# Moving one gradient store, three partial-partition stores and one weight load in a traffic-bound attention backward kernel

## The chip, the cores and the metric

The kernel runs on one core of a Trainium2 chip. The metric is the device time of one execution in microseconds (us), as the median of several runs. Each run is also told with its *span*, the time from the first to the last instruction by the profiler, about 1.8 us less than the device time.

In the profile PE is the matmul engine, DVE the vector engine, ACT the scalar engine, POOL GpSimd and SP SyncE. SPq and ACTq are the queues on which SyncE and ACT issue DMAs, and L546 is line 546 of that kernel. `[t <-DMA x]` tells that the engine stood idle for t us before, until that DMA. The *DMA engines* are the 16 units that move the bytes. A *semaphore* is a counter on which instructions wait.

A ratio below is the mean time of one kernel's runs over that of the kernel before in the same rounds on the same chip, so it is not quite the ratio of the medians that are quoted beside it. The kernel before was run 6, 11, 11, 11 and 9 times in five sessions (the last four on different chips), with medians of 404.82, 404.98, 404.67, 404.64 and 404.92 us and single runs from 403.89 to 407.32 us. Differences under about 0.2% (0.8 us) are therefore near the noise, and the text says so where it matters. Ratios of different sessions are compared with the same caution.

## The reference, cut to what matters

The reference computes a gated mix of a one-token attention over a cache and a small MLP, and all gradients of it. Shapes are of one token: x has 640 elements, there are 32 heads, and each head has a K cache and a V cache of 4096 x 128 in bfloat16 (1 MiB each).

```
q  = x @ wq                       # wq: 640 x 4096
p  = softmax(q . K / sqrt(128))   # per head
o  = p . V
a  = o @ wo                       # wo: 4096 x 640
b  = mish(x @ w1 + b1) @ w2       # w1: 640 x 1728
out = g * a + (1 - g) * b,        g = sigmoid(sum(x * gate_w))
# returned: out and the gradients of x, K, V, wq, wo, w1, b1, w2, gate_w
```

Every gradient has the shape of its input. So the kernel reads all of K, V and the weights (82.03 MB) and writes as much again. Each row of dK is a number times q, and each row of dV a number times a vector, so the arithmetic is light. The kernel is a copy machine with some work in the middle.

## The kernel before

Loads of K and V, and of the weights, are issued from SyncE (a hardware queue, q1 in the profile). Nearly all stores are issued from GpSimd (a software queue, q0), the last ones from SyncE. These are the parts that the change and the argument touch.

```
def ring(h):                                   # who issues the dK and dV stores
    return nc.sync if h >= H - 2 else nc.gpsimd
def load_wq(w):                                # a quarter of wq, 1280 KB
    ...
    nc.sync.dma_start(wqs[w][:], wq_v[...])

# start: wq piece 0, wo piece 0, K0, V0, K1, V1, wo piece 1, w1, ... all on SyncE
load_wq(0); load_wo(0); load_k(0); load_v(0); ...

def dwo():                                     # gradient of wo for four heads
    ...
    (nc.sync if g == NG - 1 else nc.gpsimd).dma_start(dwo_v[g], wos[g][:])

def dw1_part(rc):                              # gradient of w1, written over w1
    def f():
        nc.vector.tensor_scalar(w1_sb[:, rc, :], m["dh_bc"][:], x_f[:, rc:rc + 1], None, ALU.mult)
        if rc == RC - 1:
            nc.gpsimd.dma_start(dw1_v, w1_sb[:])          # 2160 KB
    return f

# in dv_half(h, 1): the store of dV of head h
if h % 10 == 9:
    spread(h // 10, dVv[h], st["dV"])          # heads 9, 19, 29
else:
    ring(h).dma_start(dVv[h], st["dV"][:])     # 128 partitions, 8 KB each

def spread(i, dst, t):                         # one dV store in three pieces
    ...
    if i == 0:
        nc.gpsimd.inc_swdge_sem([], [], mode="reset_dge_cursor")
    for a, b in (((120, 125), (0, 120), (125, 128)),
                 ((0, 14), (14, 119), (119, 128)),
                 ((0, 8), (8, 128)))[i]:
        nc.gpsimd.dma_start(out[a:b, :], src[a:b, :], max_dma_last_dim=J * Dh)

# the head loop: loads run three heads ahead
load_k(h + 3); load_v(h + 3); ...; period(h)
...
# after the last head: last pieces of dwq
nc.sync.dma_start(dwq_v[:, :, CL:], dwq_l[:])
```

`spread` needs a word. By the general rule of the Trainium skill ("DMA: Bandwidth & Descriptors", Why a DMA increments its semaphore by 16 and not by 1), a store of 128 partitions is divided over all 16 DMA engines, so 8 rows each, and a software-queue store whose partition count is divisible by 15 and not by 16 runs on 15 consecutive engines from a cursor that goes round. The page also has an exception for some direct copies on trn2. The pieces are cut so that the 120-row (or 105-row) piece leaves out the same engine each time. By the general rule the left-out engine gets 2, 2 and 1 rows in place of 8 from the three patterns, so 19 rows less in all. That is an estimate from the page's rule.

Of the kernel before, what the change touches and what calls it, by code (L numbers as in the profile page):

```python
# [16 lines left out]
def kernel(  # L17
# [24 lines left out]
    nc = tc.nc  # L42
    P = 128
    _, H, Sk, Dh = A_k_cache.shape
# [3 lines left out]
    RC = D // P  # L48
# [4 lines left out]
    WG = 8  # L53
# [14 lines left out]
    dVv = out_3.rearrange("b h (p j) d -> (b h) p j d", p=P)  # L68
    wq_v = A_wq.rearrange("(rc r) c -> r rc c", r=P)
# [4 lines left out]
    dw1_v = out_6.rearrange("(rc r) f -> r rc f", r=P)  # L74
# [38 lines left out]
    kts, vts, wqs, wos = {}, {}, {}, {}  # L113

    def ring(h):
        return nc.sync if h >= H - 2 else nc.gpsimd

    def load_k(h):
        if h < H:
            kts[h] = kv_in.tile([P, J, Dh], BF16, name="Kn", tag="Kn", bufs=KB)  # L120
            nc.sync.dma_start(kts[h][:], Kv[h])

    def load_v(h):
        if h < H:
            vts[h] = kv_in.tile([P, J, Dh], BF16, name="Vn", tag="Vn", bufs=VB)
            nc.sync.dma_start(vts[h][:], Vv[h])

    def load_wq(w):
        if w < H // WG:
            wqs[w] = wts.tile([P, RC, WG * Dh], BF16, name="wq_g", tag="wq_g")  # L130
            nc.sync.dma_start(wqs[w][:], wq_v[:, :, w * WG * Dh:(w + 1) * WG * Dh])

    def load_wo(g):
        if g < NG:
            wos[g] = wts.tile([P, G, D], BF16, name="wo_g", tag="wo_g", bufs=3)
            nc.sync.dma_start(wos[g][:], wo_v[g])
# [3 lines left out]
    def load_w2(c):  # L140
        a, b = CH[c][0], min(CH[c][1], FM)
        w2cs[c] = mlp.tile([P, 5, D], BF16, name="w2c", tag="w2c", bufs=2)
        nc.sync.dma_start(w2cs[c][:, 0:b - a, :], w2_v[:, a:b, :])

    load_wq(0)
    load_wo(0)
    load_k(0)
# [4 lines left out]
    w1_sb = mlp.tile([P, RC, F], BF16, name="w1_sb", tag="w1_sb")  # L152
# [94 lines left out]
    steps, done = [], {}  # L247

    def add(name, kind, fn, deps=(), head=0):
        steps.append((name, kind, fn, tuple(deps), head))  # L250
# [154 lines left out]
    def mlp_steps():  # L405
# [136 lines left out]
        def dw1_part(rc):  # L542
            def f():
                nc.vector.tensor_scalar(w1_sb[:, rc, :], m["dh_bc"][:], x_f[:, rc:rc + 1], None, ALU.mult)
                if rc == RC - 1:
                    nc.gpsimd.dma_start(dw1_v, w1_sb[:])  # L546
            return f

        H0 = 2
# [55 lines left out]
    def s_chunk(h, c, ts):  # L605
        gp = gps[h // G]
        if c == 0:
            sts[h] = {"A": sa_ps.tile([P, 512], F32, name="sA", tag="sA")}
        products(sts[h]["A"][:, 0:J + W], ts[c], c, gp["x2"][:, 0, h % G])

    def outer(dst, col, row, half):
        n = J // 2
        a, b = half * n, (half + 1) * n
        nc.vector.tensor_tensor(  # L614
            dst[:, a:b, :].rearrange("p j (a b) -> p j a b", b=2),
            col[:, a:b, :].unsqueeze(2).to_broadcast([P, n, Dh // 2, 2]),
            row.rearrange("p (a b) -> p a b", b=2).unsqueeze(1).to_broadcast([P, n, Dh // 2, 2]),
            ALU.mult)
# [16 lines left out]
    def dv_half(h, half):  # L635
        st = sts[h]
        if half == 0:
            st["dV"] = outs.tile([P, J, Dh], BF16, name="dV_sb", tag="dVK")
        outer(st["dV"], st["p"], gps[h // G]["qd"][:, 1, (h % G) * Dh:(h % G + 1) * Dh], half)
        if half == 1:  # L640
            if h % 10 == 9:
                spread(h // 10, dVv[h], st["dV"])
            else:
                ring(h).dma_start(dVv[h], st["dV"][:])  # L644

    def spread(i, dst, t):
        src = t[:].rearrange("p j d -> p (j d)")
        out = dst.rearrange("p j d -> p (j d)")
        if i == 0:
            nc.gpsimd.inc_swdge_sem([], [], mode="reset_dge_cursor")  # L650
        for a, b in (((120, 125), (0, 120), (125, 128)), ((0, 14), (14, 119), (119, 128)), ((0, 8), (8, 128)))[i]:
            nc.gpsimd.dma_start(out[a:b, :], src[a:b, :], max_dma_last_dim=J * Dh)

    def period(h):
# [12 lines left out]
        def o_part(a, b):  # L667
            for j in range(a, b):
# [31 lines left out]
        nc.vector.scalar_tensor_tensor(pj[:], in0=DP[:, 0:J], scalar=1.0, in1=e[:], op0=ALU.mult, op1=ALU.mult,  # L700
                                       accum_out=part[:])
        dv_half(h, 0)
        nc.tensor.transpose(PT, part[:].to_broadcast([P, P]), ident_f[:])  # L703
        if nxt:
# [6 lines left out]
        nc.vector.scalar_tensor_tensor(ds[:], in0=DP[:, 0:J].unsqueeze(2).to_broadcast([P, J, 2]), scalar=dd[:], in1=p_bf[:],  # L711
                                       op0=ALU.subtract, op1=ALU.mult)
        dv_half(h, 1)
        nc.vector.tensor_scalar(o_all[:, h:h + 1], O[:, 0:1], rz[:], None, ALU.mult)  # L714
        if nxt:
# [19 lines left out]
    dwqt = {}  # L735
    CL = (NG - 1) * GD

    def dwq_make(rc):
        def f():
            t = dwqt[rc] = kv_in.tile([P, J * Dh], BF16, name="dwq_t", tag="Kn" if rc % 2 == 0 else "Vn", bufs=KB)  # L740
            nc.vector.tensor_scalar(t[:, 0:CL], dq_bc[:, 0:CL], x_f[:, rc:rc + 1], None, ALU.mult)
        return f

    def dwq_store(rc):
        (nc.sync if rc else nc.gpsimd).dma_start(dwq_v[:, rc, 0:CL], dwqt[rc][:, 0:CL])
# [8 lines left out]
            s_chunk(0, c - 1, tk)  # L754
    s_chunk(0, NT - 1, tk)
    mlp_steps()
    for h in range(H):
        hh, g = h % G, h // G
        if hh == 3:
            assert g == 0 or f"dwo{g - 1}" in done  # L760
            load_wo(g + 2)
            if g % 2 == 0:
                assert g == 0 or f"dx{RC - 1}_{g - 1}" in done
                load_wq(g // 2 + 1)
        load_k(h + 3)
        load_v(h + 3)
        if hh == 1 and g + 1 < NG:
            rest = steps[:]
            steps.clear()
            prep_steps(g + 1, h)  # L770
            steps.extend(rest)
        if h == H - 3:
            for rc in range(RC):
                add(f"dwq{rc}", "D", dwq_make(rc), (f"dqb{NG - 2}",), h + (rc + 1) // 2)
                add(f"dwqs{rc}", "T", lambda rc=rc: dwq_store(rc), (f"dwq{rc}",), h)
        period(h)
        if hh == G - 1:
            mlp_left = steps[:]
            steps.clear()
            finish_steps(g)  # L780
            steps.extend(mlp_left)
# [7 lines left out]
    for rc in range(RC):  # L789
        nc.vector.tensor_scalar(dwq_l[:, rc, :], dq_bc[:, CL:], x_f[:, rc:rc + 1], None, ALU.mult)  # L790
    nc.sync.dma_start(dwq_v[:, :, CL:], dwq_l[:])
    assert len(dwqt) == RC

    C = lambda name, shape, dt=F32: const.tile(list(shape), dt, name=name)
# [64 lines left out]
```

## Time and profile before

| what | before |
|---|---|
| median of 3 runs, known when the prediction was made (of all 6 of that session) | 405.26 us (404.82) |
| span of the profiled run | 402.6 us |
| bytes moved, mean rate | 164.93 MB, 410 GB/s |
| PE, DVE, ACT busy | 75%, 75%, 44% of the span |

The page of the kernel before, rows of DMA: the busy share of the 16 engines in 40 slices of the span (9 is 90% or more), the rate in each, and the queues with packets, MB and their share of the 16 engines' time.

```profile
DMA  8999999999999999999999999999999999999995
GB/s 290 420 413 408 422 424 418 419 426 421 423 424 419 395 421 414 421 425 423 423 419 425 425 423 416 412 425 423 421 425 422 424 420 424 424 415 367 413 396 216
...
q1 hardware_dynamic: 16480, 91.20, 54.9%
q0 software_dynamic: 11216, 72.85, 43.7%
```

The DMA row is full from the second slice to the last but one, while no computing engine is above 75%. The kernel is bound by traffic. The dips are the first slice (290), the 37th (367) and the last two (396, 216).

The chain of waits of the kernel before, near its end (start, length, what):

```profile
332.40 0.67 POOL out_dram L631
...
333.25 0.89 POOL out_dram L546
...
336.80 25.24 DMA out_dram<-dV_sb
...
362.13 1.23 DVE dK_sb L614
```

Two lines of its table of waits (who waited for whom: us in total, times, longest), and one of the same table for SyncE's queue:

```profile
PE qc_ps L278 <- DMA wq_g<-in_A_wq_dram: 6.9, 2, 4.8
...
DVE dK_sb L614 <- DMA out_dram<-dV_sb: 3.8, 1, 3.8
```

```profile
SPq L375 <- DMA out_dram<-dV_sb: 4.9, 1, 4.9
```

L546 is the dw1 store. It is issued at 333.25 us, and the dV store behind it on the same queue, issued at 336.80 us, lands only 25 us later. DVE then finds no free output buffer and stands for 3.8 us. SyncE holds the last dwo store (L375) for 4.9 us until another store lands.

The timeline of SyncE's queue in the kernel before, from 370 us on (start, length, engine, line, what), and below it DVE's instructions that make the data of the last two stores.

```profile
370.18 0.35 SPq L644 DMA_DIRECT2D out_dram<-dV_sb  x1
...
379.46 0.33 SPq L644 DMA_DIRECT2D out_dram<-dV_sb  x1
...
391.42 0.33 SPq L375 DMA_DIRECT2D out_dram<-wo_g  x1
393.60 0.38 SPq L791 DMA_DIRECT2D out_dram<-dwq_l  x1
```

### The profile page before, as it was taken

The numbers are of one execution on the slowest core, as the hardware profiler recorded it, in microseconds if no ns is written. First come the engines' busy times: TensorE is split into PE (matmuls) and PEld (weight loads), VectorE is DVE, ScalarE is ACT, GpSimd is POOL, SyncE is SP. The second block draws the span as 40 slices with busy tenths as digits, with TensorE's granted clock in tenths as the row PEclk, the third lists the DMA queues.
The fourth block names the chain that finished last, engine by engine and source line by source line (L and its number), as shares of the span: only waits on it lengthen the run. The fifth ranks groups of instructions, "written<-read, shape, count | busy, mean of one in ns | idle before, by whom it ended". The sixth has DMA issues, their size and how long they took to land.

```text
span 402.6 us, 13606 instructions
## 1 busy us (share of the span) xinstructions
PE 300.7 (75%) x5872; PEld 271.9 (68%) x5872; DVE 303.7 (75%) x791; ACT 177.6 (44%) x411; POOL 46.5 (12%) x93
## 2 busy tenths in 40 slices
PE   0688888678888788878876988739887888966510
PEld 0577888568877778778866878628776778856500
DVE  3339666646599999977669799855999996968980
ACT  1355455325453555546523556505554555533300
POOL 0001111010011311111101113101111112121000
PEclk9999999857999999989988899957999999998755
DMA  8999999999999999999999999999999999999995
GB/s 290 420 413 408 422 424 418 419 426 421 423 424 419 395 421 414 421 425 423 423 419 425 425 423 416 412 425 423 421 425 422 424 420 424 424 415 367 413 396 216
DMA packets 27816, 164.93 MB, mean 410 GB/s; under 512 B 3164, under 2 KB 3868, under 8 KB 11884
## 3 DMA queue, kind: packets, MB, share of 16 engines
q1 hardware_dynamic: 16480, 91.20, 54.9%
q0 software_dynamic: 11216, 72.85, 43.7%
q8 instruction: 46, 0.75, 0.7%
q14 instruction: 14, 0.11, 0.1%
q10 hardware_dynamic: 60, 0.01, 0.0%
HBM read 82.03 MB, written 82.03 MB: 407 GB/s over the span
## 4 chain that ended last, share of the span: by engine, by line
DMA 35%; DVE 35%; PE 19%; ACT 4%; issue 3%; POOL 0%; ACTq 0%; SPq 0%; POOLq 0%; DVEq 0%
DMA Kn<-in_A_k_cache_dram 28%; DVE dK_sb L614 9%; PE tr L589 8%; DVE dV_sb L614 7%; DMA out_dram<-dV_sb 6%; DVE junk L385 4%; ACT tT L591 3%; PE sA L669 3%; DVE junk L288 3%; PE sA L598 2%; PE sB L722 2%; DVE junk L537 2%; DVE junk L494 1%; DMA vec_rows<-in_gate_w_dram 1%; DVE dj L709 1%
## 5 line engine op out<-in xcount | busy, mean ns | idle before, releaser
L591 ACT COPY tT<-tr 128x512 f32<-128x512 f32 x256 | 142.6, 588 | 138.9 <-PE tr L589 138.0
L598 PEld LDWEIGHTS <-tT 128*128 128x128 bf16 x2048 | 80.0, 98 | 43.9 <-ACT tT L591 33.8
L589 PE MATMUL tr<-ident_f,Kn 128*128 128x128 f32 x512 | 82.8, 300 | 12.8 <-DMA Kn<-in_A_k_cache_dram 12.8
L614 DVE TENSOR_TENSOR dK_sb<-ds_bf,qd 128x2048 bf16<-128x2048 bf16 x64 | 77.8, 1216 | 4.1 <-DMA out_dram<-dV_sb 3.8
L614 DVE TENSOR_TENSOR dV_sb<-p_bf,qd 128x2048 bf16<-128x2048 bf16 x64 | 78.0, 1218 | 0.6 <-DMA out_dram<-dK_sb 0.4
L589 PE MATMUL tr<-ident_f,Vn 128*128 128x128 f32 x512 | 74.3, 281 | 0.0
L589 PEld LDWEIGHTS tr<-ident_f,Kn 128*128 128x128 f32 x512 | 61.9, 153 | 14.2 <-issue 14.2
L598 PE MATMUL sA<-qd,tT 128*128 128x48 bf16 x1024 | 48.9, 187 | 23.4 <-ACT dq_all L727 12.7
L589 PEld LDWEIGHTS tr<-ident_f,Vn 128*128 128x128 f32 x512 | 57.3, 144 | 0.0
L598 PE MATMUL sB<-qd,tT 128*128 128x48 bf16 x1024 | 46.2, 183 | 0.0
L669 PEld LDWEIGHTS <-Vn 128*128 128x128 bf16 x1024 | 30.6, 96 | 10.6 <-issue 10.6
L669 PE MATMUL sA<-e_bf,Vn 128*128 128x48 bf16 x1024 | 31.2, 184 | 7.8 <-DVE zs L689 6.3
L631 POOL DMA_DIRECT2D out_dram<-dK_sb x30 | 17.2, 574 | 149.0 <-DVE rz L691 102.2
L722 PE MATMUL sB<-ds_bf,Kn 128*128 128x48 bf16 x1024 | 32.9, 187 | 1.4 <-DVE ds_bf L711 1.4
L673 DVE TENSOR_REDUCE m<-sA 128x1 f32<-128x32 f32 x32 | 6.0, 189 | 35.8 <-PE sA L598 29.1
L722 PEld LDWEIGHTS <-Kn 128*128 128x128 bf16 x1024 | 30.3, 99 | 1.6 <-issue 1.6
L644 POOL DMA_DIRECT2D out_dram<-dV_sb x27 | 14.6, 540 | 136.7 <-DVE o_all L714 48.1
L288 DVE SCALAR_TENSOR_TENSOR junk<-wo_g,da_bc 128x640 bf16<-128x640 bf16 x32 | 26.2, 820 | 1.7 <-ACT da_bc L229 1.1
L385 DVE SCALAR_TENSOR_TENSOR junk<-wq_g,dq_bc 128x1024 bf16<-128x1024 bf16 (+1 forms) x25 | 25.1, 1004 | 0.2
L693 ACT ACTIVATE p_bf<-e_bf,rz 128x64 bf16<-128x64 bf16 x32 | 11.1, 348 | 13.6 <-DVE rz L691 10.8
L700 DVE SCALAR_TENSOR_TENSOR pj<-sB,e_bf 128x32 f32<-128x32 f32 x32 | 6.1, 190 | 13.1 <-PE sB L598 12.9
L709 DVE TENSOR_SCALAR_CACHE_REDUCE dj<-sB,rz 128x128 f32<-128x128 f32 x32 | 11.1, 346 | 6.4 <-PE sB L703 6.4
(153 smaller groups left out, 275.4 us busy)
## 6 DMA issues: line engine op xcount, KB each, us to landing
Kn<-in_A_k_cache_dram SPq DMA_DIRECT2D x32, 1024.0 KB, 24.3
Vn<-in_A_v_cache_dram SPq DMA_DIRECT2D x32, 1024.0 KB, 28.8
out_dram<-dK_sb POOLq DMA_DIRECT2D x30, 1024.0 KB, 12.0
out_dram<-dV_sb POOLq DMA_DIRECT2D x27, 1024.0 KB, 11.3
wq_g<-in_A_wq_dram SPq DMA_DIRECT2D x4, 1280.0 KB, 19.7
wo_g<-in_A_wo_dram SPq DMA_DIRECT2D x8, 640.0 KB, 14.9
out_dram<-wo_g POOLq DMA_DIRECT2D x7, 640.0 KB, 11.6
out_dram<-dwq_t SPq DMA_DIRECT2D x4, 896.0 KB, 14.5
```

The lines of the kernel that those rows point to most:

```text
L288: nc.vector.scalar_tensor_tensor(junk[:, 0:D], in0=wos[g][:, i, :], scalar=1.0, in1=da_bc[:], op0=ALU.mult, op1=ALU.mult, accum_out=gp["do ...
L385: nc.vector.scalar_tensor_tensor(junk[:, c0:c1], in0=wqs[w][:, rc, c0:c1], scalar=1.0, in1=dq_bc[:, w * WG * Dh + c0:w * WG * Dh + c1], op ...
L589: nc.tensor.transpose(tp[:, t, :], flat[:, k * P:(k + 1) * P], ident_f[:])
L591: nc.scalar.copy(sb[:].rearrange("p a b -> p (a b)"), tp[:].rearrange("p a b -> p (a b)"))
L598: nc.tensor.matmul(out[:, 2 * k:2 * k + W], lhsT=tb[:, t, par, :], rhs=vec[:, par, :].unsqueeze(1).to_broadcast([P, W // 2, 2]), start=(pa ...
L614: nc.vector.tensor_tensor(dst[:, a:b, :].rearrange("p j (a b) -> p j a b", b=2), col[:, a:b, :].unsqueeze(2).to_broadcast([P, n, Dh // 2, 2]),
L631: ring(h).dma_start(dKv[h], st["dK"][:])
L644: ring(h).dma_start(dVv[h], st["dV"][:])
L669: nc.tensor.matmul(O, lhsT=vts[h][:, j, :], rhs=st["e"][:, j:j + 1].to_broadcast([P, W]), start=(j == 0), stop=(j == J - 1))
L693: nc.scalar.activation(p_bf[:], e[:].unsqueeze(2).to_broadcast([P, J, 2]), ACT.Copy, scale=rz[:])
L709: nc.vector.tensor_scalar(dj[:], PT, rz[:], None, ALU.mult, ALU.add, accum_out=dd[:])
L722: nc.tensor.matmul(DQ, lhsT=kts[h][:, j, :], rhs=ds[:, j, 0:1].to_broadcast([P, W]), start=(j == 0), stop=(j == J - 1))
```

## The change

The intent has three parts. The dw1 store leaves GpSimd's queue, where it holds up dK and dV stores, and goes on SyncE's queue behind the last V load, where a stretch without loads begins. The three partial-partition stores move from heads 9, 19 and 29 to 8, 17 and 26. The first piece of wq goes on ACT's ring, so that wo and K start on SyncE's at once.

```diff
@@ load_wq
-            nc.sync.dma_start(wqs[w][:], wq_v[...])
+            (nc.sync if w else nc.scalar).dma_start(wqs[w][:], wq_v[...])
@@ dw1_part
-                if rc == RC - 1:
-                    nc.gpsimd.dma_start(dw1_v, w1_sb[:])
@@ dv_half
-            if h % 10 == 9:
-                spread(h // 10, dVv[h], st["dV"])
+            if h in (8, 17, 26):
+                spread(h // 9, dVv[h], st["dV"])
@@ head loop, after load_k(h + 3) and load_v(h + 3)
+        if h + 3 == H - 1 and f"dw1_{RC - 1}" in done:
+            nc.sync.dma_start(dw1_v, w1_sb[:])
+            stored.append(1)
```

## The prediction

> **What bounds the kernel now.** Traffic. The page moves 164.93 MB in a span of 402.6 us, 410 GB/s; its DMA row reads 9 in nearly every slice, its rate row 413 to 426 GB/s in most. Packets taken one by one from the trace give 16 busy engines from about 3 us to 364 us, at 309 ns per 8 KB. The Trainium skill ("DMA: Bandwidth & Descriptors", Bandwidth) puts the ceiling at 435 GB/s; this trace agrees, never passing 427. PE and DVE (75% each) are not the bound. All packets' times over 16 engines come to 400 us, 394 if each took its undisturbed time. So at most 5 to 6 us (1.3%) is to be had.
>
> **Where those lie.** (1) Start: nothing moves before 2 us, then 258, 353, 390 GB/s; about 1.3 us lost. (2) 364 to 374 us: loads have run out, only the GpSimd queue's stores are left, the rate falls to 340 GB/s and packets take 10 to 25% longer; about 1.5 us. (3) From 390 us engines run dry one by one; four go on to 401.2 us while most ended at 396.5 to 397.7; about 3 us between the mean end and the last.
>
> **What the change does.**
> - dw1 (2,160 KB, issued on GpSimd's queue at 333.3 us, 23.7 us to landing) leaves that queue. Behind it the dV store issued at 336.8 us landed only at 362.0, the output buffers ran out, and DVE sat 3.8 us before dK at 362.1 (waits; 25 us of the chain). On SyncE's ring behind the last V load (issued 337.4, landed by 366.9) it fills the stretch where that ring is empty, so hole (2) should mostly close and the heads from 30 on come 3 to 4 us earlier. Cost: 3,456-byte packets (135 ns each, as in the w1 load) in place of 6,912-byte ones (262 ns), some 0.15 us per engine.
> - The partial-partition stores relieve one engine by 19 rows (about 5.9 us) in total, as before; only the moment changes. In the last V load one engine is 5 us behind the next (366.9 against 361.7 us); seven rows relieved earlier should bring that to about 3.
> - wq on ACT's ring: same bytes. It starts about 1.3 us later, while wo and K start at once. The first products wait for the broadcast of dy (done at 11.2 us) and wo, not for wq; worth 0 to 0.4 us.
>
> **On the critical path.** Bytes don't change and the last four engines appear to have had a backlog through the 3.8 us stall, so most of that stall is not given back: it was hidden behind queued stores. What counts is the inflated packets at 366 to 374 us (about 1 us), plus 0 to 1 us at the ends.
>
> **Prediction:** 403.6 us, range 401.2 to 405.8. Faster by over 2%: 0.02; within 2%: 0.97; slower by over 2%: 0.01.
>
> **Right if:** DVE's wait for the dV store and the 25 us DMA piece in the chain are gone; the rate from 362 to 382 us is near 410; the last dV and dK are ready 3 to 4 us earlier; yet the span shrinks by only 1 to 2 us, its tail still a few engines behind the others. **Wrong if:** the last heads wait for K or V, the rate at 364 to 374 us stays low, or the tail flattens and the whole 3 to 5 us arrive. dw1 ahead of dV and dwq stores on one ring could delay the last issues, which already wait for earlier stores (wo's last issue, 4.9 us); that would eat the gain.

## More of the kernel before

In the kernel before, the last engine ends the first piece of head 29's store 5.7 us behind the median of the 16, and the second piece 3.7 us behind it: 2.0 us less, where seven rows of 309 ns make 2.2 us.

The stretches of the kernel before, 362 to 376 us and from 388 us on. The columns are the stretch, its length, the busy time of PE, PE's weight loads, DVE, ACT and POOL, the granted clock, the DMA share and the rate.

```profile
362.00:376.00 14.00, 10.39 (x205) 9.63 (x205) 11.82 (x22) 6.02 (x14) 1.75 (x2) 0.88 0.98 376
388.00:402.60 14.60, 0.28 (x1) 0.09 (x1) 4.34 (x16) 0.26 (x1) 0.00 (x0) 0.50 0.67 266
```

```profile
384.51 1.27 DVE L374 TENSOR_SCALAR wo_g<-da_bc,o 128x640 bf16<-128x640 bf16 x4
385.69 1.40 DVE L790 TENSOR_SCALAR dwq_l<-dq_bc,cols_f 128x512 bf16<-128x512 bf16 x5
```

The last dwo store is ready at 385.8 us and issued at 391.4 us.

## The result, and the profile after

The changed kernel measured 404.91 us (404.61 to 405.39, 6 runs) against 404.82 us (404.18 to 406.43, 6 runs). The ratio is 1.0000, with a 95% interval of 0.998 to 1.0019. The span is 402.8 us against 402.6 us.

The page of the changed kernel, the same rows. ACT's ring is q10.

```profile
DMA  8999999999999999999999999999999999999984
GB/s 306 404 420 391 417 423 416 424 421 423 421 422 420 425 421 400 419 427 421 421 423 422 423 421 418 423 423 425 422 422 424 425 419 416 421 419 417 424 367 179
...
q1 hardware_dynamic: 16480, 92.10, 55.5%
q0 software_dynamic: 10880, 70.64, 42.1%
q10 hardware_dynamic: 716, 1.32, 0.9%
```

The same stretches of the changed kernel:

```profile
362.00:376.00 14.00, 10.87 (x240) 9.59 (x240) 12.98 (x27) 5.62 (x14) 1.75 (x2) 0.97 1.02 420
388.00:402.60 14.60, 0.28 (x1) 0.09 (x1) 0.43 (x3) 0.26 (x1) 0.00 (x0) 0.50 0.56 222
```

The dip at 362 to 376 us is gone: 420 in place of 376 GB/s. What was moved there is missing later: 222 in place of 266 GB/s from 388 us on. DVE, which still had 4.34 us of work after 388 us, now has 0.43 us. The computing is done 4 us sooner and nothing comes of it.

Waits of the changed kernel, those of all engines first and then those of SyncE's queue. The wait of DVE for a dV store is no longer in the table.

```profile
PE qc_ps L278 <- DMA wq_g<-in_A_wq_dram: 19.9, 3, 9.5
```

```profile
SPq L375 <- DMA out_dram<-dV_sb: 8.9, 1, 8.9
```

The timeline of SyncE's queue in the changed kernel, and below it DVE's instructions that make the data of the last two stores:

```profile
340.21 0.88 SPq L767 DMA_DIRECT2D out_dram<-w_sb  x1
366.19 0.34 SPq L642 DMA_DIRECT2D out_dram<-dV_sb  x1
...
375.36 0.33 SPq L642 DMA_DIRECT2D out_dram<-dV_sb  x1
...
391.83 0.33 SPq L375 DMA_DIRECT2D out_dram<-wo_g  x1
394.21 0.38 SPq L793 DMA_DIRECT2D out_dram<-dwq_l  x1
```

```profile
380.40 1.26 DVE L374 TENSOR_SCALAR wo_g<-da_bc,o 128x640 bf16<-128x640 bf16 x4
381.58 1.39 DVE L792 TENSOR_SCALAR dwq_l<-dq_bc,cols_f 128x512 bf16<-128x512 bf16 x5
```

The last dV store is issued 4.1 us earlier (375.36 against 379.46 us), and the data of the last two stores is ready 4.1 us earlier. Yet they are issued 0.4 and 0.6 us *later*.

An account of the DMA engines shows where the time went. It is worked out from the start, length and size of every DMA packet in the trace. *Idle* is the missing busy time of the 16 engines, divided by 16.2 (packets overlap a little, so a full load reads 16.2). *Slow* is what packets took above the usual time of their size (309 ns for 8 KB), divided by 16.

```
us of all 16 engines        2.5-40      40-355     355-362    362-376     376-388    388-end
                          idle slow   idle slow   idle slow   idle slow   idle slow   idle slow
before                    0.07 1.21   0.00 4.09   0.00 0.19   0.53 1.10   0.00 0.24   4.80 0.18
after                     0.00 1.56   0.00 3.93   0.00 0.10   0.00 0.20   0.00 0.08   6.64 0.08
```

The change takes 1.43 us of idle and slow time out of 362 to 376 us. It gives back 1.84 us as idle time after 388 us.

A second account tells why. Each of these DMAs leaves 16 marks on its semaphore in the trace, one for each engine that has finished its part. So the trace tells when each of the 16 engines finished each load or store, though not which engine it was.

```
                 last V load: all landed   last engine behind   last store (dwq_l): all landed   last engine behind
                                           the next                                              the next / the median
before                366.9 us               5.2 us                   401.5 us                     0.1 / 3.0 us
after                 361.0 us               3.5 us                   401.7 us                     2.8 / 4.3 us
```

In both kernels one engine is behind all others by the end of the loads. In the kernel before, the others then lose their lead. Most of that goes with the partial-partition store of head 29, of which they carry more rows: its first piece leaves the last engine 3.3 us behind the next (372.6 us), its second 0.5 us (373.5 us). By the landing of the dV store issued at 370.18 us the last engine is 0.0 us behind the next. The hole of 362 to 376 us may have added to this, but two runs that are told below show that it isn't needed and doesn't do it alone. `dw1_only` has that store and no idle time in the stretch, and its last engine goes from 5.6 us behind at the last V load to 0.3 us at the end. `stores_only` has 0.68 us of idle time there and no such store, and goes from 2.2 to 2.3 us. In the changed kernel the store has left the stretch and the hole is filled, so the fast engines keep their lead and end early. The last one goes on to 401.7 us as before. Its landings there (dK in two halves, dwo, dwq) come 1.2 to 1.6 us apart, at 397.4, 398.6, 400.1 and 401.7 us. That is the time of its own packets: 8 of 159 ns, 8 of 196 ns, 40 of 46 ns that overlap slightly. It has no gaps to close.

The stores of heads 8, 17 and 26 act on this same engine. In the changed kernel it was 1.9 us behind the next at 124.8 us, and 0.2 us or less from 130.8 to 139.1 us, after the store of head 8.

### The profile page after: what moved, and what is told of

It is laid out like the page before. It is cut to its first block, busy times and chain, and to the rows that moved or that the text cites. A ratio compares the mean times of both kernels' runs of the same rounds, so it can differ in the third digit from the quotient of the medians.

```text
span 402.8 us, 13607 instructions
## 1 busy us (share of the span) xinstructions
PE 291.9 (72%) x5872; PEld 264.1 (66%) x5872; DVE 302.8 (75%) x791; ACT 177.2 (44%) x411; POOL 45.6 (11%) x92
## 4 chain that ended last, share of the span: by engine, by line
DVE 37%; DMA 26%; PE 24%; ACT 7%; issue 3%; ACTq 0%
DMA Kn<-in_A_k_cache_dram 21%; DVE dV_sb L612 9%; DVE dK_sb L612 9%; PE tr L587 9%; ACT tT L589 6%; DMA wq_g<-in_A_wq_dram 5%; DVE junk L385 5%; PE sA L667 4%; PE sA L596 3%; PE sB L720 3%; DVE junk L288 2%; DVE junk L537 2%; DVE wo_g L374 1%; DVE junk L494 1%; DVE dj L707 1%
## 5 line engine op out<-in xcount | busy, mean ns | idle before, releaser
L596 PEld LDWEIGHTS <-tT 128*128 128x128 bf16 x2048 | 78.9, 97 | 41.1 <-ACT tT L589 35.3
L587 PE MATMUL tr<-ident_f,Kn 128*128 128x128 f32 x512 | 79.3, 291 | 8.9 <-DMA Kn<-in_A_k_cache_dram 8.9
L587 PE MATMUL tr<-ident_f,Vn 128*128 128x128 f32 x512 | 72.5, 277 | 0.0
L587 PEld LDWEIGHTS tr<-ident_f,Kn 128*128 128x128 f32 x512 | 59.3, 148 | 9.9 <-issue 9.9
L587 PEld LDWEIGHTS tr<-ident_f,Vn 128*128 128x128 f32 x512 | 55.9, 141 | 0.0
L720 PE MATMUL sB<-ds_bf,Kn 128*128 128x48 bf16 x1024 | 31.4, 184 | 1.4 <-DVE ds_bf L709 1.4
L720 PEld LDWEIGHTS <-Kn 128*128 128x128 bf16 x1024 | 28.8, 96 | 1.6 <-issue 1.6
L278 PE MATMUL qc_ps<-cols_bf,wq_g 128*128 128x1 bf16 x160 | 5.3, 164 | 19.9 <-DMA wq_g<-in_A_wq_dram 19.9
L278 PEld LDWEIGHTS <-wq_g 128*128 128x128 bf16 x160 | 4.7, 99 | 20.4 <-DMA wq_g<-in_A_wq_dram 20.4
```

The lines of the kernel that those rows point to most:

```text
L278: nc.tensor.matmul(qc_ps[:, hh:hh + 1], lhsT=wq[:, rc, off + hh * Dh:off + (hh + 1) * Dh], rhs=x_bf[:, rc:rc + 1], start=(rc == 0), stop=( ...
L587: nc.tensor.transpose(tp[:, t, :], flat[:, k * P:(k + 1) * P], ident_f[:])
L596: nc.tensor.matmul(out[:, 2 * k:2 * k + W], lhsT=tb[:, t, par, :], rhs=vec[:, par, :].unsqueeze(1).to_broadcast([P, W // 2, 2]), start=(pa ...
L720: nc.tensor.matmul(DQ, lhsT=kts[h][:, j, :], rhs=ds[:, j, 0:1].to_broadcast([P, W]), start=(j == 0), stop=(j == J - 1))
```

## The experiments

Three explanations were put against each other. **Slowest engine:** the end is the backlog of the one DMA engine that is last in every load, and time freed on the other fifteen is worth nothing. **Late issue:** the last two stores are issued too late, because SyncE's issue waits for the landing of an earlier store (391.83 us is when the last engine of the last dV store landed, 391.8 us; 394.21 follows a dwq store's 394.1 us), and this eats the gain. The trace shows the wait itself: just before each of the two issues SyncE waits on the semaphore (104 and 105) on which that store and the earlier one both count. **Late wq:** two parts gain and the third gives it back. Every run below gave correct results, and each was timed in five rounds against the kernel before.

One slip: the expectations say that wq landed "at 19.9 us". The 19.9 is PE's total wait for pieces of wq; the first piece landed at 20.6 us. And the first store of the changed kernel comes at 36.2 us against 29.1 us, so 7 us later and not 12.

### One part alone: dw1_only and stores_only

`dw1_only` is the kernel before with the two dw1 edits of the diff alone. `stores_only` is the kernel before with the edit in `dv_half` alone.

```diff
# dw1_only
-                    nc.gpsimd.dma_start(dw1_v, w1_sb[:])
+            nc.sync.dma_start(dw1_v, w1_sb[:])      # behind the last V load
# stores_only
-            if h % 10 == 9:
-                spread(h // 10, dVv[h], st["dV"])
+            if h in (8, 17, 26):
+                spread(h // 9, dVv[h], st["dV"])
```

> The kernel before with dw1 alone moved behind the last V load. Slowest-engine theory (the end is the work queued on the one DMA engine that lands last in every load; time freed on the other fifteen is worth nothing): DVE's 3.8 us wait before dK goes, the rate from 364 to 374 us is above 405 GB/s, and the span still lies within 1 us of 402.6. Late-wq theory (dw1 gains 1.5 us and the late wq, landing at 19.9 in place of 7.1 us, gives it back): 1 to 2 us faster than before, ratio about 0.996.

> The kernel before with the three partial-partition stores alone moved to heads 8, 17 and 26. Slowest-engine theory: the same work on the same engine, so within 0.5 us of before; the last V load's last engine is about 3 us behind the next in place of 5.2. Prediction's own term: 0 to 1 us faster.

`dw1_only` measured 403.99 us (6 runs) against 404.98 us, ratio 0.9971 (0.9948 to 0.9994). `stores_only` measured 403.98 us, ratio 0.9974 (0.9949 to 0.9999). Each is about 1 us faster, at the edge of the noise, and together with wq nothing is left. DVE's wait went with dw1 alone, and 362 to 376 us ran at 410 GB/s. By the spans of the profiled runs the slowest-engine theory held (402.4 and 402.3 against 402.6 us), but that 402.6 us is of another session. In this one the median span was 403.1 us before and 402.2 us for each of the two. By it `dw1_only` still lies within the 1 us that was allowed, which does not tell the theories apart; "within 0.5 us of before" for `stores_only` was a miss; and the medians are nearer the late-wq theory. The last V load of `stores_only` has its last engine 2.2 us behind the next (expected about 3). This called for the next pair.

A second finding is in the account of packets. In `stores_only` dw1 is still on GpSimd's queue and the stretch from 362 to 376 us still has idle time (0.68 us), but its slow time is 0.25 us in place of 1.10 us. In the six kernels with a partial-partition store at head 29 (before, `dw1_only`, `wq_only` and the three `relief4` kernels that have one there), packets in that stretch are slow by 0.45 to 1.39 us; in the changed kernel and `dw1_and_stores`, which have none there, by 0.20 and 0.19 us. The 4 KB packets of that store take 172 to 205 ns on the mean, and 159 to 164 ns in the same kernels' partial-partition stores at heads 8 to 26. So the slow packets came with the partial-partition store falling among stores, and not with the loads' end alone.

### The wq part: dw1_and_stores and wq_only

`dw1_and_stores` is the changed kernel with wq back on SyncE. `wq_only` is the kernel before with wq's first piece on ACT's ring.

```diff
# dw1_and_stores, against the changed kernel
-            (nc.sync if w else nc.scalar).dma_start(wqs[w][:], wq_v[...])
+            nc.sync.dma_start(wqs[w][:], wq_v[...])
# wq_only, against the kernel before: the reverse
```

> The changed kernel without its third part: wq back on SyncE. If the wq part gives back what the other two gained (each alone 1.0 us faster than before, all three together 0), this is 0.8 to 1.5 us faster than the changed kernel: about 403.5 to 404.1, ratio to before about 0.997. If the parts dw1 and stores merely don't add up and wq is neutral, it measures about 404.9, ratio about 1.0. Slowest-engine theory adds: the last engine still ends 2 to 3 us behind the next.

> The kernel before with the first wq piece alone on ACT's ring. Late-wq theory: wq lands near 20 us in place of 7.1, the first store comes some 12 us later, and the time rises by 0.5 to 1.5 us, ratio about 1.002 to 1.004. Prediction's term: 0 to 0.4 us faster. Slowest-engine theory alone: no change, within 0.3 us.

`dw1_and_stores` measured 404.25 us (5 runs) against 404.67 us, ratio 0.9984 (0.9966 to 1.0002). `wq_only` measured 405.14 us, ratio 1.0016 (0.9994 to 1.0037). The sign is that of the late-wq theory, the size about half of it: 0.16% in each pairing (1.0000 against 0.9984, which are of two sessions, and 1.0016 against 1). Both intervals reach 1. The two other parts do not add up: each alone 0.26 to 0.29%, both together 0.16%. And in `dw1_and_stores`, as expected, the last engine still ends 2.7 us behind the next, at 401.5 us.

What happened to wq is plain. PE's timeline and SyncE's queue in the kernel before:

```profile
11.20 0.67 PE L278 MATMUL qc_ps<-cols_bf,wq_g 128*128 128x1 bf16 x20
```

```profile
0.73 0.44 SPq L131 DMA_DIRECT2D wq_g<-in_A_wq_dram  x1
```

PE's timeline and ACT's queue in the changed kernel:

```profile
20.68 0.69 PE L278 MATMUL qc_ps<-cols_bf,wq_g 128*128 128x1 bf16 x20 [9.46 <-DMA wq_g<-in_A_wq_dram]
```

```profile
1.97 0.43 ACTq L131 DMA_DIRECT2D wq_g<-in_A_wq_dram  x1
```

The wq piece, issued at 1.97 us in place of 0.73 us, needed until 20.6 us in place of 7.1 us. From 8 to 16 us ACT's ring moved 82 to 97 GB/s while SyncE's moved 320 to 332 GB/s. wq's packets have 2 KB and those of K and V 8 KB. The Trainium skill ("DMA: Bandwidth & Descriptors", Queues, rings and completion order) says that an engine goes round its queues packet by packet; this trace agrees: from 8 to 16 us 317 packets of 8 KB started on SyncE's queue and 349 of 2 KB on ACT's, and the rates are near 1 to 4. Here the two rings got nearly equal turns, and so not equal bytes.

### Relief of the last engine: after_relief4 and before_relief4

`after_relief4` adds a fourth partial-partition store at head 29 to the changed kernel. `before_relief4` adds one to the kernel before. Both use the pattern with the cursor reset for it, which by the page's rule takes 6 rows off the left-out engine.

```diff
# after_relief4, against the changed kernel
-            if h in (8, 17, 26):
-                spread(h // 9, dVv[h], st["dV"])
+            if h in {8: 0, 17: 1, 26: 2, 29: 0}:
+                spread({8: 0, 17: 1, 26: 2, 29: 0}[h], dVv[h], st["dV"])
# before_relief4, against the kernel before: {9: 0, 19: 1, 26: 2, 29: 0}
```

> The changed kernel with a fourth partial-partition store, at head 29, which takes 6 more rows (12 packets of 159 ns, 1.9 us) off the engine that lands last. Slowest-engine theory: that engine ends 1.9 us earlier and the whole kernel with it: span about 401, ratio about 0.995; the last engine of the last stores about 1 us behind the next in place of 2.9. Late-issue theory (the last two stores are issued at 391.8 and 394.2 us although their data is ready at 381.7 and 383.0, because their issue waits for a store eight places earlier on the hardware queue): no gain by itself but for what the earlier landing brings forward, under 1 us.

> The kernel before with one more partial-partition store (heads 9, 19, 26, 29), so 6 rows or 1.9 us less for the same engine. In the kernel before four engines end together (400.7 to 401.2 us), in the changed kernel one ends 2.8 us behind the rest. Slowest-engine theory: here taking work from one of four gains at most 0.5 us, where the same store gained 1.3 to 1.6 us on the changed kernel. Rival (any relief of this engine speeds the loads and so the whole kernel): the same 1.3 to 1.6 us as there, ratio about 0.996.

`after_relief4` measured 403.28 us (6 runs) against 404.98 us, ratio 0.9959 (0.9936 to 0.9983); its span is 401.5 us. The last store landed at 400.4 us, with the last engine 0.0 us behind the next in place of 2.8 us (expected about 1 us, and a gain of 1.9 us). So 1.3 us of span came of one store that moves no byte less. The slow packets at 362 to 376 us came back with that store, about 1.2 us of them by the account above, as many as in the kernel before (1.10), and the kernel is faster all the same. `before_relief4` measured 404.13 us (5 runs) against 404.67 us, ratio 0.9985 (0.9965 to 1.0004): 0.5 us, as the slowest-engine theory said, against 1.6 us for the same store there. The intervals overlap, so the pair speaks for the theory and does not prove it. Also, in the one profile of `before_relief4` the last engine is 1.2 us behind the next, so the picture of four engines tied did not repeat exactly. Which engine was last there is not known.

### Earlier issue of the last stores: after_last_gpsimd

```diff
-            (nc.sync if g == NG - 1 else nc.gpsimd).dma_start(dwo_v[g], wos[g][:])
+            nc.gpsimd.dma_start(dwo_v[g], wos[g][:])
-    nc.sync.dma_start(dwq_v[:, :, CL:], dwq_l[:])
+    nc.gpsimd.dma_start(dwq_v[:, :, CL:], dwq_l[:])
```

> The changed kernel with its last dwo and dwq stores issued from GpSimd, whose queue has been free since 363 us, in place of SyncE. Late-issue theory: both are issued by 384 us, the engines stay full to about 394 us and the end comes about 2 us earlier, ratio about 0.995. Slowest-engine theory: they are issued by 384 us, fifteen engines end sooner, the last engine has the same work and ends within 0.5 us of 401.4: ratio 0.999 to 1.001.

It measured 404.80 us (6 runs) against 404.98 us, ratio 0.9991 (0.9967 to 1.0015); the changed kernel's was 1.0000. The issue did come early, as POOL's timeline of this run shows:

```profile
382.63 0.61 POOL L375 DMA_DIRECT2D out_dram<-wo_g  x1 [18.18 <-DVE wo_g L374]
383.94 0.89 POOL L793 DMA_DIRECT2D out_dram<-dwq_l  x1 [0.70 <-DVE ambj L803]
```

SyncE's queue in the same run, with both halves of the last dK:

```profile
378.99 4.32 SPq L627 DMA_DIRECT2D out_dram<-dK_sb  x2
```

The last packets of the two moved stores ended at 395.8 us. What landed last was the second half of the last dK, at 402.2 us, issued from SyncE at about the same time as they were, with the last engine 2.7 us behind the next. Issuing 9 to 10 us sooner moved the end by nothing that can be measured. The late-issue theory falls: the wait in SyncE's queue was the shadow of the last engine's backlog, not its cause.

### More relief, and where it is put

`no_wq_relief4` is `after_relief4` with wq on SyncE. The `early` kernels are `dw1_and_stores` with other heads for the partial-partition stores, all before the loads end. The last two have the edit of `after_last_gpsimd` too, and the last has wq on ACT's ring again.

```diff
# against dw1_and_stores: head -> pattern
-            if h in (8, 17, 26):
+            if h in {8: 0, 17: 1, 26: 2, 29: 0}:           # no_wq_relief4
+            if h in {5: 0, 12: 1, 19: 2, 26: 0}:           # early_relief4
+            if h in {4: 0, 9: 1, 14: 2, 20: 0, 26: 1}:     # early_relief5 and the two behind it
```

> dw1 and the stores at heads 8, 17 and 26 moved, wq left on SyncE, and a fourth partial-partition store at head 29. If the effects of relief (1.3 to 1.6 us on the changed kernel) and of wq (about 0.9 us) add: about 402.4 us, ratio about 0.993 to 0.994. If they don't: 403.3 as with wq on ACT.

> dw1 behind the last V load, wq on SyncE, four partial-partition stores at heads 5, 12, 19 and 26, none where only stores are left. If such a store costs extra only when it lands after the loads have ended (its 4,096-byte packets took 190 to 205 ns on the mean at head 29, 160 ns at heads up to 26), packets at 362 to 376 us take their undisturbed time and the last engine ends about 1.9 us before the 401.2 us of dw1_and_stores, so near 399.3: about 402.4 us, 0.5 to 0.8 us under no_wq_relief4. Rival: the place doesn't matter and the time is that of no_wq_relief4, 403.1.

> As early_relief4 with five stores, at heads 4, 9, 14, 20 and 26: 12 rows (3.8 us) less for the engine that is 2.7 us behind the next in dw1_and_stores. Slowest-engine theory: the gain stops at the next engines, which ended at 398.5 us, so a last packet at 398.6 to 399.2 us and 401.8 to 402.4 us, at most 0.6 us better than early_relief4. Rival (the engine's share of work goes on paying): another 1.9 us, 400.5 us.

> early_relief5 with the last dwo and dwq stores on GpSimd's queue. With the slow engine out of the way, the last two stores' issue (at 391 to 394 us on SyncE, data ready by 383 us) may now set the end. If so: 1 to 2 us faster than early_relief5. If the engines that end last still have a backlog then: within 0.3 us.

> early_relief5_gpsimd (ratio 0.9936) with the first wq piece on ACT's ring again. Late-wq theory (the late piece costs about 0.5 us, as wq_only at 1.0016 and the changed kernel at 1.0000 against dw1_and_stores at 0.9984 suggest, each within its noise): ratio 0.9945 to 0.996. Neutral wq: 0.993 to 0.994.

| kernel | median us (runs) | ratio (95%) | last store landed, last engine behind the next, behind the median |
|---|---|---|---|
| no_wq_relief4 | 403.06 (6) | 0.9955 (0.9935 to 0.9976) | 400.6, 0.1, 1.9 |
| early_relief4 | 402.88 (6) | 0.9963 (0.9947 to 0.9979) | 400.0, 0.9, 2.7 |
| early_relief5 | 402.07 (5) | 0.9940 (0.9928 to 0.9952) | 399.1, 0.1, 1.4 |
| early_relief5_gpsimd | 401.72 (6) | 0.9936 (0.9921 to 0.9950) | 398.9, 0.1, 1.2 |
| early_relief5_gpsimd_wq | 402.78 (5) | 0.9943 (0.9929 to 0.9956) | 400.4, 1.1, 3.0 |

`no_wq_relief4` came out between its two expectations. `early_relief4` has 0.12 us of slow packets at 362 to 376 us where `no_wq_relief4` has 1.39 us. Its last landing was to be near 399.3 us and came at 400.0. By the last landing it is 0.6 us ahead of `no_wq_relief4`, but by the ratio it isn't (one of its runs took 404.59 us), so the gain of the earlier place is seen in the profile and not in the time. `early_relief5` does as the slowest-engine theory said: the fifth store brings the last engine level with the next (0.9 to 0.1 us behind), and the gain is about 0.8 us, near the 0.6 us that was allowed and not the rival's 1.9 us. `early_relief5_gpsimd` is the fastest of all, 401.72 against 404.64 us, but its last edit adds only 0.3 us, within noise. With wq on ACT's ring the last engine is 1.1 us behind again, and the ratio is 0.07% worse, inside the intervals and between the two expectations. The time of wq thus has the same sign in three pairings and is significant in none.

The same two stretches in the best version, `early_relief5_gpsimd`, whose span is 399.8 us (columns as above):

```profile
362.00:376.00 14.00, 7.85 (x185) 6.96 (x181) 12.46 (x24) 4.28 (x11) 0.00 (x0) 0.87 1.02 422
388.00:402.60 14.60, 0.00 (x0) 0.00 (x0) 0.00 (x0) 0.00 (x0) 0.00 (x0) 0.53 0.49 205
```

The first stretch is full (422 GB/s). The second is short of 222 GB/s only because the kernel ends 2.8 us before the stretch does, and no engine computes in it any more. Some imbalance is left: the last store on SyncE's queue still lands over 8.6 us from the first of the 16 engines to the last.

## Why the prediction was right or wrong

- **"Same", 403.6 us, 401.2 to 405.8.** The class was right and 404.91 us lies in the range. The prediction started from 405.26 us, the median of three runs; the 1.7 us below it did not come, for the changed kernel's median equals that of the kernel before in the same session. Landing in the range says little for the mechanism: the time of the kernel before lies in it too. By the prediction's own test ("the span shrinks by only 1 to 2 us") it missed, as the span grew by 0.2 us.
- **Bound by traffic, at most 5 to 6 us to be had.** Right as far as tried: the best version took 2.9 us of it. The bound itself is loose: 402.6 less the 394 us of undisturbed packets is 8.6 us, and 5 to 6 us is the sum of the three holes alone. "Never passing 427" holds for the page's slices of 10 us (426 at most); over 2 us the packets come to as much as 430 GB/s.
- **dw1 leaves the queue, DVE's 3.8 us and the 25 us of the chain go, the hole closes, the last dV and dK are ready 3 to 4 us sooner.** Right in all: the wait is gone, 420 in place of 376 GB/s, 4.1 us.
- **"Most of that stall is not given back: it was hidden behind queued stores."** Right; in the full change it was nothing at all. `dw1_only`, which moves dw1 alone and so takes the stall away, measured 0.29% faster, at the edge of the noise, and why is not known.
- **"What counts is the inflated packets at 366 to 374 us (about 1 us), plus 0 to 1 us at the ends."** This is the step that failed. The 1 us was a mean over 16 engines, and the end belongs to one. The packets were there, and they were removed (1.10 to 0.20 us), but the time was lost by engines that had a lead to lose. The last engine had a backlog through it all. The prediction had this very fact in the sentence before (four engines with a backlog) and still counted the mean. The runs put in its place: 1.43 us freed at 362 to 376 us turns into 1.84 us of idle after 388 us, while rows taken off the last engine bring 1.3 us of span at once, with the slow packets back in the stretch (`after_relief4`).
- **The cause of the slow packets.** The prediction named the store-only stretch. `stores_only` has that stretch too, with 0.25 us; the slow ones came with the partial-partition store of head 29 in it.
- **The stores' new heads bring the last engine from 5.2 to about 3 us behind.** Right, 3.5 us. That it is worth no time of its own followed from the same total of rows; alone it measured 0.26% faster, which is not explained.
- **wq "worth 0 to 0.4 us".** Wrong in sign by all three pairings (0.07 to 0.16% slower), though none is beyond noise and two of the three span sessions. Its reason was wrong for certain: PE waited 9.5 us for wq, because on its own ring it landed at 20.6 us and not 1.3 us late. Why a late start of the computing should cost time in a kernel bound by traffic stays open. The landings suggest that the last engine bears it (401.5 against 402.1 us for `wq_only`).
- **dw1 could delay the last issues.** They were later (8.9 against 4.9 us of wait), but `after_last_gpsimd` shows that this costs nothing.

What also stays open is why one engine has more to do than the rest. Instruction fetches (46 packets of 16 KB on q8) would be a candidate, but the trace does not tell which engine carried them.

## What to carry to other kernels

When DMA bounds a kernel, ask how far the last of the 16 engines is behind the others, and read it from the landings of each transfer. In the changed kernel a hole that the other fifteen had was no loss, and filling it bought nothing. Taking a few rows off the engine that is last went with 0.3 to 0.4% here (`after_relief4` against the changed kernel, `no_wq_relief4` and `early_relief5` against `dw1_and_stores`), whereas a visible stall of the computing engines, removed in the full change, paid nothing. Of these three pairs only the second is of one session; the intervals of the third alone do not overlap. The load that was moved to a second ring shared by packets here: with small packets beside large ones it got the smaller part and came late.

## What the Trainium skill lacked or had wrong

- "DMA: Bandwidth & Descriptors", Queues, rings and completion order: it speaks of turns by packet but not of what follows for two rings with different packets. Here 2 KB packets on ACT's ring got 82 to 97 GB/s beside 320 to 332 GB/s of 8 KB packets, and a load took from 1.97 to 20.6 us in place of 0.73 to 7.1 us.
- The same page, Latency and other measured facts, says that some engines are usually slower. It does not tell how far behind such an engine comes, nor what that costs at the end of a kernel; whether the last engine here is one of those it names, no trace shows. Here one engine was 5.2 us behind the next at the last V load, 2.8 us at the end of the changed kernel, and taking rows off it gained 1.3 us of span.
- The same page, on how many engines a transfer takes, doesn't say what such a partial-partition store costs. Here its 4 KB packets took 159 to 164 ns on the mean beside loads, and 172 to 205 ns at head 29, where it fell into the stretch in which the loads had ended.
- No page has that an issue may have to wait for the landing of an earlier store because both count on one semaphore. Here two stores were issued 10 and 11 us after their data was ready, at the moment when an earlier store of the same queue had landed on its last engine (391.83 after 391.8 us, 394.21 after 394.1 us). Just before each issue the trace has SyncE waiting on the semaphore of that earlier store.
